# Fused block attention, MLP and mixture of experts: every maximum, exponential, copy and group of turns of the attention as a task of its own

## The chip, the cores and the metric

The kernel runs on one core of a Trainium2 chip. The metric is device time in microseconds, the median of several runs; lower is better. TensorE (PE), VectorE (DVE), ScalarE (ACT), GpSimd (POOL) and the DMA queue of SyncE (SP) run side by side, each through its own instructions in order, and wait for each other at semaphores. TensorE writes PSUM alone: eight banks of 128 x 512 f32 here.

## The reference, cut to what matters

```python
def _attn_ref(q, k, v):                   # 4 batches, 8 heads, 576 tokens, 64 features
    scores = np.matmul(q, k.transpose(0, 1, 3, 2)) / np.sqrt(D)
    scores = np.where(block_i >= block_j, scores, -1e9)     # blocks of 64 tokens
    attn = np.exp(scores - scores.max(-1))
    return np.matmul(attn / (attn.sum(-1) + 1e-09), v)
x = attention as (2304, 512)
x = leaky_relu(x @ w_in) @ w_out                            # 512 -> 2048 -> 512, weights are float64
P = 8 rounds of row and column normalisation of exp(x @ w_gate - max)
out = sum over 8 experts of P[:, e] * (relu(x @ w1[e]) @ w2[e])
```

## The kernel before, in words

Attention works on pairs of heads: 16 pairs p, two heads of 64 features side by side on the 128 partitions. Query blocks i = 0 to 8 of 64 tokens see keys 0 to 64(i + 1). For a pair, `scores(p, ...)` makes the products of some query blocks in banks of `ps_sc` (four banks; block 8 takes two, the others one), VectorE takes the negated row maxima into `nmax`, and ScalarE writes the exponentials to `ex` with their row sums to `ssum`. `turn_attn(p, g)` then transposes `ex` on TensorE in seven groups g, four 128x128 turns in a bank of `ps_tr` (two banks; group 6 is one turn, in `av`), and copies them to `at`: on VectorE for g = 1 and 5, on ScalarE for the others. `weigh(p, c, ...)` multiplies `at` by chunk c of the values into `av` (one buffer of two banks): `first_product` is chunk 0, `other_parts` are chunks 1 to 4. `split_x(p)` divides by the row totals (two VectorE products with `by_feature`) and splits the result in a high part (ScalarE cast) and a low part (GpSimd). The totals take a way through DRAM: `totals` (GpSimd, a VectorE reciprocal, two `row` DMAs) and `spread_totals` (four DMAs that read `row` back, spread over partitions, to `by_feature`).

`turn_q`, `turn_k` and `turn_tail` transpose the queries and keys of a later pair in banks of `ps_tr`; `spread` copies them to `qT` on ScalarE, `place_k` to `kT` on VectorE.

The loop over p is a software pipeline. In round p the list `turns` names the work in order: `prv` is pair p - 1, `cur` p, `nxt` p + 1 (scores) and `fol` p + 2 (turns of q and k). Attention stands in `manual_schedule` for TensorE, VectorE and ScalarE: these three run it in the program's order, and GpSimd and SP in an order that a planner sets. Each helper traces its products, maxima, exponentials and copies together, so the list's order is that of whole helpers.

Beside it, `steps` are the 72 steps that turn the first dense weights from float64 to two f32 parts: a load, six VectorE steps, one ScalarE step, two GpSimd instructions in one step, for each of eight units. One is taken behind each `scores`, five a round. After attention come the dense layers, which TensorE's queue may begin between the last rounds' instructions.

Of the kernel before, what the change touches and what calls it, by code (L numbers as in the profile page):

```python
# [8 lines left out]
F32 = mybir.dt.float32  # L9
F32R = mybir.dt.float32r  # L10
U32 = mybir.dt.uint32
AF = mybir.ActivationFunctionType
ALU = mybir.AluOpType
AX = mybir.AxisListType

P = 128
BLK = 64
# [19 lines left out]
def block_attention_mlp_moe(  # L37
# [15 lines left out]
    nc = tc.nc  # L53
    B, H, S, D = q.shape
# [3 lines left out]
    NQ = S // BLK  # L58
# [8 lines left out]
    TAIL = S - NFULL * P  # L67
# [147 lines left out]
    def attention(att, ps_sc, ps_tr, ps_av):  # L215
# [11 lines left out]
        off = [P * sum(nch[:i]) for i in range(NQ)]  # L227
        ew = P * sum(nch)
        ex = [att.tile([P, ew], F32, name=f"ex{i}") for i in range(2)]
        nmax = [att.tile([P, NQ + 1], F32, name=f"nmax{i}") for i in range(2)]  # L230
        ssum = [att.tile([P, NQ + 1], F32, name=f"ssum{i}") for i in range(2)]
        rsum = [att.tile([P, 2, (NQ + 1) // 2], F32, name=f"rsum{i}") for i in range(2)]
        NPAR = ((NQ + 1) // 2, NQ // 2)
        by_feature = [[att.tile([P, BLK * n], F32, name=f"by_feature{i}{n}") for n in NPAR] for i in range(2)]
        xs = att.tile([P, S], F32, name="xs")
# [38 lines left out]
        W = NFULL * P  # L274

        def spread(p, src, lo, n):
            scale = 1.0 / float(D) ** 0.5
            nc.scalar.activation(
                out=qT[p % 2][:, lo * BLK:(lo + n) * BLK], in_=src[:, 0:n * BLK], func=AF.Copy, scale=scale
            )  # L280

        def place_k(p, src, lo, hi):
            nc.vector.tensor_copy(out=kT[p % 2][:, lo:hi], in_=src)  # L283

        av = {}

        def av_tile(p):
            if p not in av:
                av[p] = ps_av.tile([P, 1024], F32, name="av", tag="av")
            return av[p]  # L290

        def turn_q(p):
            qm = ps_tr.tile([P, 512], F32, name="qm", tag="tr")
            for t in range(NFULL):
                nc.tensor.transpose(qm[:, t * P:(t + 1) * P], qraw[:, t, :], ident)
            spread(p, qm, 0, W // BLK)

        def turn_k(p):
            km = ps_tr.tile([P, 512], F32, name="km", tag="tr")
            for t in range(NFULL):  # L300
                nc.tensor.transpose(km[:, t * P:(t + 1) * P], kraw[:, t, :], ident)
            place_k(p, km[:, 0:W], 0, W)

        def turn_tail(p):
            tail = ps_tr.tile([P, 512], F32, name="qk_tail", tag="tr")
            nc.tensor.transpose(tail[:, 0:2 * TAIL], tails, ident)
            spread(p, tail, W // BLK, TAIL // BLK)
            place_k(p, tail[:, TAIL:2 * TAIL], W, S)

        latest = [None]
        crossed = range(1, NQ, 2)

        def scores(p, *members):
            nm, sm = nmax[p % 2], ssum[p % 2]
            work = []
            for i in members:
                n = BLK * (i + 1)
                cuts = [(0, n)] if n <= 512 else [(0, n // 2), (n // 2, n)]  # L320
                work.append((i, [
                    (lo, hi, ps_sc.tile([P, 512], F32, name="sc", tag="sc")[:, 0:hi - lo]) for lo, hi in cuts
                ]))
            for i, parts in work:
                for lo, hi, sc in parts:
                    for h in range(2):
                        r, o = slice(h * D, (h + 1) * D), (1 - h if i in crossed else h) * BLK
                        nc.tensor.matmul(  # L328
                            sc[o:o + BLK, :], qT[p % 2][r, i * BLK:(i + 1) * BLK], kT[p % 2][r, lo:hi],
                            start=True, stop=True,  # L330
                        )
            for i, parts in work:
                for s, (lo, hi, sc) in enumerate(parts):
                    latest[0] = nc.vector.tensor_reduce(  # L334
                        out=nm[:, i + s:i + s + 1], in_=sc, axis=AX.X, op=ALU.max, negate=True
                    )
                x = nm[:, i:i + 1]
                if len(parts) > 1:
                    nc.vector.tensor_tensor(out=x, in0=x, in1=nm[:, i + 1:i + 2], op=ALU.min)
                for s, (lo, hi, sc) in enumerate(parts):  # L340
                    nc.scalar.activation(  # L341
                        out=ex[p % 2][:, off[i] + lo:off[i] + hi], in_=sc, func=AF.Exp,
                        bias=x, scale=1.0, accum_out=sm[:, i + s:i + s + 1],
                    )
                if len(parts) > 1:
                    nc.gpsimd.tensor_tensor(
                        out=sm[:, i:i + 1], in0=sm[:, i:i + 1], in1=sm[:, i + 1:i + 2], op=ALU.add
                    )

        rows = {}  # L350

# [20 lines left out]
        def turn_attn(p, g):  # L372
            todo = order[4 * g:4 * g + 4]
            n = len(todo)
            if n == 1:
                tr = av_tile(p)[:, P:2 * P].rearrange("p (s h q) -> p s h q", s=1, h=2)
            else:
                tr = ps_tr.tile([P, 4, 2, BLK], F32, name="tr", tag="tr")
            for s, (i, c) in enumerate(todo):
                nc.tensor.transpose(  # L380
                    tr[:, s].rearrange("p h q -> p (h q)"),
                    ex[p % 2][:, off[i] + c * P:off[i] + (c + 1) * P],
                    swap if i in crossed else ident,
                )
            dst = at[:, 4 * g:4 * g + n]
            if g not in (1, 5):
                nc.scalar.copy(out=dst, in_=tr[:, 0:n])  # L387
            else:
                nc.vector.tensor_copy(out=dst, in_=tr[:, 0:n])

        o = 512 - P

        def weigh(p, c, h, part):
# [6 lines left out]
            else:  # L400
# [3 lines left out]
                    start=c == 0, stop=c == NKC - 1,  # L404
                )

        def split_x(p):
            b, hp = divmod(p, NPAIR)
            t = av.pop(p)
            for c, n in enumerate(NPAR):  # L410
                nc.vector.tensor_tensor(  # L411
                    out=xs.rearrange("p (i q) -> p i q", q=BLK)[:, c:NQ:2],
                    in0=t[:, o:o + S].rearrange("p (i q) -> p i q", q=BLK)[:, c:NQ:2],
                    in1=by_feature[p % 2][c].rearrange("p (q i) -> p i q", i=n), op=ALU.mult,
                )
            t0, t1 = b * S, (b + 1) * S
            cuts = [t0, XCUT, t1] if t0 < XCUT < t1 else [t0, t1]
            for u0, u1 in zip(cuts, cuts[1:]):
                hi, lo = x_parts(hp, u0, u1)
                y = xs[:, u0 - t0:u1 - t0]  # L420
                nc.scalar.copy(out=hi, in_=y)  # L421
                nc.gpsimd.tensor_tensor(out=lo, in0=y, in1=f32(hi), op=ALU.subtract)
# [7 lines left out]
        def first_product(p):  # L430
            for f, *a in first_part:
                f(p, *a)

        turns = [
            ("nxt", scores, 8), ("cur", turn_attn, 0), *other_parts[0:2],
            ("nxt", scores, 3, 2), *other_parts[2:], ("nxt", load_v), ("cur", turn_attn, 1), ("prv", split_x),
            ("nxt", scores, 5, 4), ("cur", totals), ("cur", turn_attn, 2), ("fol", turn_q),
            ("nxt", scores, 1, 0), ("fol", turn_tail), ("cur", first_product), ("cur", turn_attn, 3),
            ("nxt", scores, 7, 6), ("fol", turn_k), ("cur", turn_attn, 4), ("cur", turn_attn, 5),
            ("cur", turn_attn, 6), ("cur", spread_totals),  # L440
        ]
        opening = [
            ("nxt", scores, 1, 0), ("nxt", scores, 3, 2), ("nxt", scores, 5, 4), ("nxt", scores, 8),
            ("fol", turn_q), ("nxt", scores, 7, 6), ("nxt", load_v), ("fol", turn_k), ("fol", turn_tail),
        ]

        nc.gpsimd.memset(still, 0.0)
# [9 lines left out]
                nc.gpsimd.tensor_copy(out=t[:, off[i] + BLK * (i + 1):off[i] + P * nch[i]], in_=nought[:, 0:BLK])  # L457
        for t in vraw:
            nc.gpsimd.tensor_copy(out=t[TAIL:, NFULL, :], in_=nought[TAIL:, :])
        turn_q(0)  # L460
        turn_k(0)
        turn_tail(0)
        warm(ps_sc, "sc", 3)
        load_qk(1)
        steps = bits_list(
# [1 line left out]
        )  # L467
        for p in range(-1, NP + 1):
            who = {"prv": p - 1, "cur": p, "nxt": p + 1, "fol": p + 2}
            if p == NP:  # L470
                first_product(p - 1)
            for w, f, *a in (turns if p >= 0 else opening):
                if 0 <= who[w] < NP and (f is not first_product or p < NP - 1):
                    f(who[w], *a)
                if f is scores and p >= 0 and steps:
                    with ExitStack() as queued:
                        if p + 1 < NP:
                            queued.enter_context(tc.issue_after(getattr(latest[0], "ins", latest[0])))
                        steps.pop(0)()
            if p + 3 < NP:  # L480
                load_qk(p + 3)
        assert not steps
# [873 lines left out]
```

## Time and profile before

| | |
|---|---|
| median of 3 runs | 2120.01 us (2118.21 to 2121.92) |
| the profiled execution's own time | 2123.31 us |
| its span | 2121.5 us |
| TensorE busy, of the span | 2063.2 us (97%) |
| VectorE, ScalarE, GpSimd busy | 1551.9, 823.8, 655.1 us |
| chain that ended last | PE 90%, DVE 4%, ACT 2% |

The shares are means over stages: attention ends at about 257 us, the rest is dense layers and experts. What an edit of attention is worth is read from its rounds, not from these shares. A TensorE row's length is modelled and overlaps the next one; the distance between starts is the time that a step takes.

### The profile page before, as it was taken

The numbers are of one execution on the slowest core, as the hardware profiler recorded it, in microseconds if no ns is written. First come the engines' busy times: TensorE is split into PE (matmuls) and PEld (weight loads), VectorE is DVE, ScalarE is ACT, GpSimd is POOL, SyncE is SP. The second block draws the span as 40 slices with busy tenths as digits, with TensorE's granted clock in tenths as the row PEclk, the third lists the DMA queues.
The fourth block names the chain that finished last, engine by engine and source line by source line (L and its number), as shares of the span: only waits on it lengthen the run. The fifth ranks groups of instructions, "written<-read, shape, count | busy, mean of one in ns | idle before, by whom it ended". The sixth has DMA issues, their size and how long they took to land.

```text
span 2121.5 us, 32380 instructions
## 1 busy us (share of the span) xinstructions
PE 2063.2 (97%) x11498; PEld 1850.6 (87%) x11498; DVE 1551.9 (73%) x2671; ACT 823.8 (39%) x1811; POOL 655.1 (31%) x639
## 2 busy tenths in 40 slices
PE   8878899999999999999999999999999999999999
PEld 4444489898889889899989999999999999999998
DVE  5566465656555977887788688888888688888886
ACT  5555433222234544454445333323233423333322
POOL 2212222213102445544552223333232332333322
PEclk9999999999999999999999999999999999999999
DMA  5333211111004978888889777777777777777772
GB/s 125 83 94 88 65 46 40 41 40 50 30 23 177 334 271 309 307 295 302 322 303 350 268 256 253 273 255 266 258 252 272 261 258 253 253 273 256 270 252 110
DMA packets 240609, 436.92 MB, mean 206 GB/s; under 512 B 80680, under 2 KB 121640, under 8 KB 240192
## 3 DMA queue, kind: packets, MB, share of 16 engines
q1 hardware_dynamic: 239248, 434.56, 59.5%
q8 instruction: 91, 1.49, 0.3%
q14 instruction: 70, 0.57, 0.1%
q10 hardware_dynamic: 1200, 0.30, 0.1%
HBM read 308.82 MB, written 125.95 MB: 205 GB/s over the span
## 4 chain that ended last, share of the span: by engine, by line
PE 90%; DVE 4%; ACT 2%; issue 1%; DMA 1%; POOL 1%; SPq 0%; POOLq 0%; DVEq 0%; ACTq 0%
PE h_ps L851 28%; PE o L1019 20%; PE o L1075 12%; PE h_ps L508 9%; PE o L528 9%; PE o L851 3%; PE av L402 2%; PE sc L328 2%; PE tr L380 2%; DVE nmax L334 1%; ACT ex L341 1%; DVE xs L411 1%; DVE kT L283 0%; ACT at L387 0%; ACT xhfirst L421 0%
## 5 line engine op out<-in xcount | busy, mean ns | idle before, releaser
L948 DVE TENSOR_TENSOR xa<-o,xa 128x384 f32<-128x384 f32 x392 | 215.9, 552 | 110.9 <-PE o L1019 106.9
L851 PE MATMUL h_ps<-xhS,w1h 128*128 128x384 f32 x768 | 257.5, 335 | 0.0
L851 PE MATMUL h_ps<-xhS,w1l 128*128 128x384 f32 x768 | 256.6, 334 | 0.0
L851 PE MATMUL h_ps<-xlS,w1h 128*128 128x384 f32 x768 | 256.6, 334 | 0.0
L948 POOL TENSOR_TENSOR xa<-xa 128x384 f32<-128x384 f32 x92 | 106.0, 1153 | 407.8 <-DVE xa L948 370.5
L948 ACT COPY places<-h_ps 128x384 f32<-128x384 f32 x192 | 92.3, 481 | 286.9 <-PE h_ps L851 219.4
L948 ACT CAST xllate<-xa 128x384 fp32r<-128x384 f32 x120 | 61.6, 513 | 279.6 <-POOL xa L948 279.6
L851 PE MATMUL h_ps<-xhA,w1h 128*128 128x384 f32 x448 | 150.7, 336 | 1.7 <-DVE c L868 1.7
L851 PE MATMUL h_ps<-xhA,w1l 128*128 128x384 f32 x448 | 149.9, 335 | 0.0
L851 PE MATMUL h_ps<-xlA,w1h 128*128 128x384 f32 x448 | 149.9, 335 | 0.0
L851 PEld LDWEIGHTS h_ps<-xhS,w1h 128*128 128x128 f32 x768 | 144.2, 188 | 0.7 <-issue 0.6
L851 PEld LDWEIGHTS h_ps<-xlS,w1h 128*128 128x128 f32 x768 | 144.2, 188 | 0.0
L851 PEld LDWEIGHTS h_ps<-xhS,w1l 128*128 128x128 f32 x768 | 144.1, 188 | 0.0
L1075 PE MATMUL o<-w2h,xhlate 128*128 128x512 f32 x408 | 143.8, 391 | 0.0
L948 POOL TENSOR_TENSOR places<-places 128x384 f32<-128x384 f32 x60 | 61.0, 1017 | 251.2 <-DVE wa L948 234.2
L1075 PE MATMUL o<-w2h,xllate 128*128 128x512 f32 x384 | 133.9, 389 | 0.0
L1019 PE MATMUL o<-xllate,w2h 128*128 128x384 f32 x480 | 122.6, 336 | 0.0
L1019 PE MATMUL o<-xhlate,w2h 128*128 128x384 f32 x480 | 121.8, 334 | 0.0
L765 POOL TENSOR_TENSOR wa<-wraw 128x256 f32<-128x256 f32 x32 | 29.0, 907 | 299.7 <-DVE w1l L783 262.9
L516 DVE TENSOR_TENSOR g<-h_ps,g 128x512 f32<-128x512 f32 (+1 forms) x80 | 50.8, 635 | 91.6 <-ACT g L515 91.3
L528 PE MATMUL o<-hh,w2h 128*128 128x512 f32 (+1 forms) x320 | 117.8, 369 | 0.0
L528 PE MATMUL o<-hh,w2l 128*128 128x512 f32 (+1 forms) x320 | 117.7, 368 | 0.0
(257 smaller groups left out, 5719.7 us busy)
## 6 DMA issues: line engine op xcount, KB each, us to landing
wraw<-in_moe_w_dram SPq DMA_DIRECT2D x64, 512.0 KB, 4.5
w1h<-k_1h SPq DMA_DIRECT2D x64, 512.0 KB, 5.1
w1l<-k_1l SPq DMA_DIRECT2D x64, 512.0 KB, 6.3
w2h<-k_1h SPq DMA_DIRECT2D x60, 512.0 KB, 6.1
w2l<-k_1l SPq DMA_DIRECT2D x60, 512.0 KB, 6.9
w1h<-k_0h SPq DMA_DIRECT2D x64, 384.0 KB, 4.1
w1l<-k_0l SPq DMA_DIRECT2D x64, 384.0 KB, 4.7
w2h<-k_0h SPq DMA_DIRECT2D x60, 384.0 KB, 3.9
```

The lines of the kernel that those rows point to most:

```text
L328: nc.tensor.matmul(sc[o:o + BLK, :], qT[p % 2][r, i * BLK:(i + 1) * BLK], kT[p % 2][r, lo:hi], start=True, stop=True,)
L334: latest[0] = nc.vector.tensor_reduce(out=nm[:, i + s:i + s + 1], in_=sc, axis=AX.X, op=ALU.max, negate=True)
L380: nc.tensor.transpose(tr[:, s].rearrange("p h q -> p (h q)"), ex[p % 2][:, off[i] + c * P:off[i] + (c + 1) * P], swap if i in crossed else ...
L402: nc.tensor.matmul(av[p][r, 512 + P * max(c - 1, 0):512 + S - P], lhsT, a[:, q0:, :], start=c == 0, stop=c == NKC - 1,)
L508: nc.tensor.matmul(ps[:, 0:n], w[:, c, cols], x, start=c == 0 and s == 0, stop=c == KC - 1 and s == 2,)
L516: nc.vector.tensor_tensor(out=g[:, 0:n], in0=ps[:, 0:n], in1=g[:, 0:n], op=ALU.max)
L528: nc.tensor.matmul(ps[:, 0:n], w[:, cut], h[:, 0:n], start=start and m == 0, stop=stop and m == 2)
L765: nc.gpsimd.tensor_tensor(out=one[:, 0], in0=a21, in1=a22, op=ALU.add)
L851: mm = nc.tensor.matmul(ps, w[:, c], x[:, c], start=first and c == 0 and s == 0, stop=c == 1 and s == 2, skip_group_check=True,)
L948: ins = f(*a, **k)
L1019: mm = nc.tensor.matmul(o, a, b, start=i == 0, stop=i == 5)
L1075: mm = nc.tensor.matmul(o, h, w, start=m == 0, stop=m == 11)
```

## The change

Helpers are cut in two: one that fills a bank and one that takes it (`turn_q` and `take_q`, `turn_attn` and `take_attn`, `score_products` and `peak`, `peak_whole`, `weights`; `split_x` gives its two products to `scale_x`). The list `turns` names each by itself, in a new order; `turn_k` stands right behind `turn_q`, ahead of `first_product`. Group 0 is turned after group 1, group 5 before group 4. `convert` stands at five places of its own. The last pair's `first_product` stands in its own round like the others. The opening keeps its order through `block` and `take_turns`.

```diff
+        held = {}
         def turn_q(p):
-            qm = ps_tr.tile([P, 512], F32, name="qm", tag="tr")
+            qm = held["q"] = ps_tr.tile([P, 512], F32, name="qm", tag="tr")
             ...
-            spread(p, qm, 0, W // BLK)
+        def take_q(p):
+            spread(p, held.pop("q"), 0, W // BLK)
...
+        def take_k(p):
+            place_k(p, held.pop("k")[:, 0:W], 0, W)
...
+        def take_q_tail(p):
+            spread(p, held["tail"], W // BLK, TAIL // BLK)
+        def take_k_tail(p):
+            place_k(p, held.pop("tail")[:, TAIL:2 * TAIL], W, S)
...
+        def peak(p, i, s=0):
+            latest[0] = nc.vector.tensor_reduce(
+                out=nmax[p % 2][:, i + s:i + s + 1], in_=score[i][s][2], axis=AX.X, op=ALU.max, negate=True
+            )
+        def peak_whole(p, i):
+            x = nmax[p % 2][:, i:i + 2]
+            nc.vector.tensor_tensor(out=x[:, 0:1], in0=x[:, 0:1], in1=x[:, 1:2], op=ALU.min)
+        def weights(p, i, s=0):
+            lo, hi, sc = score[i][s]
+            sm = ssum[p % 2]
+            nc.scalar.activation(
+                out=ex[p % 2][:, off[i] + lo:off[i] + hi], in_=sc, func=AF.Exp,
+                bias=nmax[p % 2][:, i:i + 1], scale=1.0, accum_out=sm[:, i + s:i + s + 1],
+            )
+            if s:
+                nc.gpsimd.tensor_tensor(out=sm[:, i:i + 1], in0=sm[:, i:i + 1], in1=sm[:, i + 1:i + 2], op=ALU.add)
...
+        def take_attn(p, g):
+            tr = held.pop(("tr", g))
+            dst = at[:, 4 * g:4 * g + tr.shape[1]]
             if g not in (1, 5):
-                nc.scalar.copy(out=dst, in_=tr[:, 0:n])
+                nc.scalar.copy(out=dst, in_=tr)
             else:
-                nc.vector.tensor_copy(out=dst, in_=tr[:, 0:n])
+                nc.vector.tensor_copy(out=dst, in_=tr)
...
+        def convert(p):
+            if steps:
+                with tc.issue_after(getattr(latest[0], "ins", latest[0])):
+                    steps.pop(0)()
         turns = [
-            ("nxt", scores, 8), ("cur", turn_attn, 0), *other_parts[0:2],
-            ("nxt", scores, 3, 2), *other_parts[2:], ("nxt", load_v), ("cur", turn_attn, 1), ("prv", split_x),
-            ("nxt", scores, 5, 4), ("cur", totals), ("cur", turn_attn, 2), ("fol", turn_q),
-            ("nxt", scores, 1, 0), ("fol", turn_tail), ("cur", first_product), ("cur", turn_attn, 3),
-            ("nxt", scores, 7, 6), ("fol", turn_k), ("cur", turn_attn, 4), ("cur", turn_attn, 5),
-            ("cur", turn_attn, 6), ("cur", spread_totals),
+            ("nxt", score_products, 8), *other_parts[0:2], ("nxt", peak, 8, 1), ("nxt", peak, 8, 0),
+            ("cur", convert), ("nxt", score_products, 3, 2), ("nxt", peak_whole, 8), ("nxt", peak, 2),
+            ("cur", turn_attn, 1), ("nxt", weights, 8, 0), ("nxt", weights, 8, 1), ("nxt", weights, 2),
+            ("cur", totals), ("cur", take_attn, 1), *other_parts[2:], ("nxt", load_v), ("cur", turn_attn, 0),
+            ("cur", turn_attn, 2), ("cur", take_attn, 0), ("nxt", score_products, 5, 4), ("cur", convert),
+            ("prv", scale_x, 0), ("nxt", peak, 3), ("fol", turn_q), ("cur", take_attn, 2), ("prv", scale_x, 1),
+            ("nxt", peak, 4), ("nxt", weights, 3), ("fol", take_q), ("fol", turn_k), ("nxt", peak, 5),
+            ("fol", take_k), ("nxt", weights, 4), ("cur", convert), ("cur", first_product),
+            ("nxt", score_products, 1, 0), ("nxt", weights, 5), ("fol", turn_tail), ("nxt", peak, 0),
+            ("cur", turn_attn, 3), ("nxt", peak, 1), ("cur", convert), ("fol", take_q_tail),
+            ("nxt", score_products, 7, 6), ("nxt", weights, 0), ("fol", take_k_tail), ("cur", turn_attn, 5),
+            ("cur", take_attn, 3), ("nxt", weights, 1), ("prv", split_x), ("cur", convert),
+            ("cur", turn_attn, 4), ("nxt", peak, 6), ("nxt", peak, 7), ("nxt", weights, 6),
+            ("cur", take_attn, 5), ("nxt", weights, 7), ("cur", take_attn, 4), ("cur", turn_attn, 6),
+            ("cur", take_attn, 6),
+            ("cur", spread_totals),
         ]
```

## Rows read from the trace of the kernel before

**Rows 1.** The page, its first line.
```profile
span 2121.5 us, 32380 instructions
```

**Rows 2.** Stretches: length, busy PE, PEld, DVE, ACT, POOL, PEclk, DMA share, GB/s.
```profile
14.34:26.42 12.08, 10.02 (x83) 5.54 (x83) 7.12 (x20) 7.76 (x26) 0.74 (x3) 1.00 0.54 127
26.42:241.64 215.22, 172.16 (x1275) 87.95 (x1274) 126.30 (x279) 117.01 (x375) 45.59 (x57) 0.91 0.37 88
241.64:256.58 14.94, 12.44 (x90) 5.73 (x90) 7.13 (x17) 7.51 (x25) 4.17 (x4) 0.89 0.27 70
256.58:300.00 43.42, 43.42 (x221) 34.32 (x222) 21.30 (x39) 16.24 (x30) 9.02 (x9) 1.00 0.10 27
```

**Rows 3.** TensorE's waits, 26.42 to 241.64 us: total, times, longest.
```profile
PE qk_tail L306 <- ACT at L387: 27.8, 13, 2.6
PE tr L380 <- DVE kT L283: 15.3, 13, 1.5
```

**Rows 4.** Busy time in two rounds, columns as in rows 2.
```profile
167.89:184.50 16.61, 13.47 (x98) 6.93 (x98) 10.25 (x23) 8.82 (x30) 2.22 (x4) 0.90 0.29 69
184.50:199.44 14.94, 11.92 (x98) 6.33 (x99) 9.26 (x23) 9.34 (x31) 4.92 (x7) 1.00 0.49 119
```

**Rows 5.** Timeline of ScalarE: start us, us, instruction, idle before.
```profile
182.13 0.51 ACT L421 CAST xhfirst<-xs 128x384 fp32r<-128x384 f32 x1 [2.16 <-DVE xs L411]
...
183.87 0.58 ACT L387 COPY at<-tr 128x512 f32<-128x512 f32 x1
```

**Rows 6.** Timeline of VectorE: the maxima of blocks 7 and 6.
```profile
187.59 1.22 DVE L334 TENSOR_REDUCE nmax<-sc 128x1 f32<-128x512 f32 x2 [1.11 <-PE sc L328]
```

**Rows 7.** Timeline of TensorE in the round at clock 1.00.
```profile
184.50 0.33 PE L306 MATMUL qk_tail<-ident,tails 128*128 128x128 f32 x1 [2.12 <-ACT at L387]
184.76 0.44 PE L399 MATMUL av<-at,vraw 128*64 128x128 f32 x4
...
185.88 0.33 PE L380 MATMUL tr<-swap,ex 128*128 128x128 f32 x1
...
186.47 1.08 PE L328 MATMUL sc<-kT,qT 64*64 64x512 f32 x8
...
190.16 1.19 PE L328 MATMUL sc<-kT,qT 64*64 64x288 f32 x8
191.28 0.33 PE L380 MATMUL tr<-ident,ex 128*128 128x128 f32 x1
...
191.87 0.97 PE L402 MATMUL av<-at,vraw 128*64 128x448 f32 x4
192.77 0.65 PE L328 MATMUL sc<-kT,qT 64*64 64x256 f32 x8
193.35 1.20 PE L402 MATMUL av<-at,vraw 128*64 128x320 f32 x12
194.48 0.33 PE L380 MATMUL tr<-ident,ex 128*128 128x128 f32 x1
...
195.07 0.86 PE L328 MATMUL sc<-kT,qT 64*64 64x384 f32 x8
195.86 0.44 PE L380 MATMUL tr<-ident,ex 128*128 128x128 f32 x2
...
196.35 0.60 PE L295 MATMUL qm<-ident,qraw 128*128 128x128 f32 x4
196.88 0.44 PE L328 MATMUL sc<-kT,qT 64*64 64x128 f32 x8
```

**Rows 8.** ScalarE's exponentials, 26.42 to 241.64 us: busy, mean ns, idle before.
```profile
L341 ACT ACTIVATE ex<-sc,nmax 128x288 f32<-128x288 f32 (+8 forms) x130 | 64.1, 501 | 43.5 <-DVE nmax L334 21.7 <-DVE nmax L339 19.9 <-DVE wb L176 1.9
```

**Rows 9.** Timelines of GpSimd and VectorE, where they meet.
```profile
160.10 1.29 POOL L202 TENSOR_TENSOR w2l<-wa,wraw 128x512 fp32r<-128x512 f32 x1
...
160.34 1.06 DVE L339 TENSOR_TENSOR nmax<-nmax 128x1 f32<-128x1 f32 x1
```

**Rows 10.** DMA issues, 26.42 to 241.64 us: count, size, median us to landing.
```profile
by_feature<-row SPq DMA_DIRECT2D x26, 80.0 KB, 2.8
```

More of the change, by code (lines that the diff above doesn't have):

```diff
@@ L290, in av_tile, with score_products @@
             return av[p]
+        held = {}
         def turn_q(p):
-            qm = ps_tr.tile([P, 512], F32, name="qm", tag="tr")
+            qm = held["q"] = ps_tr.tile([P, 512], F32, name="qm", tag="tr")
             for t in range(NFULL):
                 nc.tensor.transpose(qm[:, t * P:(t + 1) * P], qraw[:, t, :], ident)
-            spread(p, qm, 0, W // BLK)
+        def take_q(p):
+            spread(p, held.pop("q"), 0, W // BLK)
         def turn_k(p):
-            km = ps_tr.tile([P, 512], F32, name="km", tag="tr")
+            km = held["k"] = ps_tr.tile([P, 512], F32, name="km", tag="tr")
             for t in range(NFULL):
                 nc.tensor.transpose(km[:, t * P:(t + 1) * P], kraw[:, t, :], ident)
-            place_k(p, km[:, 0:W], 0, W)
+        def take_k(p):
+            place_k(p, held.pop("k")[:, 0:W], 0, W)
         def turn_tail(p):
-            tail = ps_tr.tile([P, 512], F32, name="qk_tail", tag="tr")
+            tail = held["tail"] = ps_tr.tile([P, 512], F32, name="qk_tail", tag="tr")
             nc.tensor.transpose(tail[:, 0:2 * TAIL], tails, ident)
-            spread(p, tail, W // BLK, TAIL // BLK)
-            place_k(p, tail[:, TAIL:2 * TAIL], W, S)
+        def take_q_tail(p):
+            spread(p, held["tail"], W // BLK, TAIL // BLK)
+        def take_k_tail(p):
+            place_k(p, held.pop("tail")[:, TAIL:2 * TAIL], W, S)
         latest = [None]
         crossed = range(1, NQ, 2)
-        def scores(p, *members):
-            nm, sm = nmax[p % 2], ssum[p % 2]
-            work = []
+        score = {}
+        def score_products(p, *members):
             for i in members:
@@ L320, in scores @@
                 cuts = [(0, n)] if n <= 512 else [(0, n // 2), (n // 2, n)]
[L321 to L325, printed above, removed]
+                score[i] = [(lo, hi, ps_sc.tile([P, 512], F32, name="sc", tag="sc")[:, 0:hi - lo]) for lo, hi in cuts]
+            for i in members:
+                for lo, hi, sc in score[i]:
                     for h in range(2):
@@ L331, in scores @@
                         )
[L332 to L348, printed above, removed]
+        def peak(p, i, s=0):
[14 more added lines that the diff above has]
+                nc.gpsimd.tensor_tensor(out=sm[:, i:i + 1], in0=sm[:, i:i + 1], in1=sm[:, i + 1:i + 2], op=ALU.add)
         rows = {}
@@ L384, in turn_attn @@
                 )
-            dst = at[:, 4 * g:4 * g + n]
+            held["tr", g] = tr[:, 0:n]
+        def take_attn(p, g):
+            tr = held.pop(("tr", g))
+            dst = at[:, 4 * g:4 * g + tr.shape[1]]
             if g not in (1, 5):
-                nc.scalar.copy(out=dst, in_=tr[:, 0:n])
+                nc.scalar.copy(out=dst, in_=tr)
             else:
-                nc.vector.tensor_copy(out=dst, in_=tr[:, 0:n])
+                nc.vector.tensor_copy(out=dst, in_=tr)
         o = 512 - P
@@ L405, in weigh, with scale_x @@
                 )
+        def scale_x(p, c):
+            n = NPAR[c]
+            nc.vector.tensor_tensor(
+                out=xs.rearrange("p (i q) -> p i q", q=BLK)[:, c:NQ:2],
+                in0=av[p][:, o:o + S].rearrange("p (i q) -> p i q", q=BLK)[:, c:NQ:2],
+                in1=by_feature[p % 2][c].rearrange("p (q i) -> p i q", i=n), op=ALU.mult,
+            )
+            if c:
+                del av[p]
         def split_x(p):
             b, hp = divmod(p, NPAIR)
[L409 to L415, printed above, removed]
             t0, t1 = b * S, (b + 1) * S
@@ new lines, in attention, with block @@
+            ("cur", spread_totals),
+        ]
+        def block(*members):
+            takes = [("nxt", score_products, *members)]
+            for i in members:
+                takes.append(("nxt", peak, i))
+                if i == NQ - 1:
+                    takes += [("nxt", peak, i, 1), ("nxt", peak_whole, i)]
+                takes.append(("nxt", weights, i))
+                if i == NQ - 1:
+                    takes.append(("nxt", weights, i, 1))
+            return takes
+        take_turns = [("fol", turn_q), ("fol", take_q)], [
+            ("fol", turn_k), ("fol", take_k), ("fol", turn_tail), ("fol", take_q_tail), ("fol", take_k_tail)
@@ L441, in attention @@
         ]
         opening = [
-            ("nxt", scores, 1, 0), ("nxt", scores, 3, 2), ("nxt", scores, 5, 4), ("nxt", scores, 8),
-            ("fol", turn_q), ("nxt", scores, 7, 6), ("nxt", load_v), ("fol", turn_k), ("fol", turn_tail),
+            *block(1, 0), *block(3, 2), *block(5, 4), *block(8), *take_turns[0], *block(7, 6), ("nxt", load_v),
+            *take_turns[1],
         ]
@@ L459, in attention @@
             nc.gpsimd.tensor_copy(out=t[TAIL:, NFULL, :], in_=nought[TAIL:, :])
-        turn_q(0)
-        turn_k(0)
-        turn_tail(0)
+        for f in (turn_q, take_q, turn_k, take_k, turn_tail, take_q_tail, take_k_tail):
+            f(0)
         warm(ps_sc, "sc", 3)
@@ L469, in attention @@
             who = {"prv": p - 1, "cur": p, "nxt": p + 1, "fol": p + 2}
-            if p == NP:
-                first_product(p - 1)
             for w, f, *a in (turns if p >= 0 else opening):
-                if 0 <= who[w] < NP and (f is not first_product or p < NP - 1):
+                if 0 <= who[w] < NP:
                     f(who[w], *a)
[L475 to L479, printed above, removed]
             if p + 3 < NP:
```

## The prediction

> **What bounds the kernel now.** I first read the page's first line, then the busy times of stretches, to find what the edited stage is worth. The profiled execution took 2123.31 us by its own time, 1.8 us more than its span [rows 1], and stands 3.30 us above the median of the runs, 2120.01. The edit touches attention alone. From 256.58 us on TensorE has no idle time (43.42 us busy of 43.42 [rows 2]), and it does the dense layers in its order until the end. So a microsecond taken out ahead of 256.58 us should come off the end, and one taken off another engine is worth nothing by itself.
>
> In attention the steady stretch is 26.42 to 241.64 us: thirteen rounds of the pair loop (p = 1 to 13), 215.22 / 13 = 16.56 us each. TensorE is busy for 13.24 us of a round, VectorE for 9.72, ScalarE for 9.00, GpSimd for 3.51, and TensorE's granted clock averages 0.91 [rows 2]. No engine is full, so something waits. The list of TensorE's waits has only two entries, each once in every round [rows 3]: `qk_tail` for a ScalarE copy, 27.8 us in all (2.14 a round), and a transpose for VectorE's copy of `kT`, 15.3 us in all (1.18). Together 3.32 us a round.
>
> The third loss is the clock. Set two rounds side by side, each from one `qk_tail` to the next [rows 4]: at mean clock 0.90 a round took 16.61 us, at 1.00 it took 14.94 with the same instructions, so a fall to the lower level (1.2 GHz) costs 1.67 us. The falls come after the wait for `qk_tail`. In the round at 1.00 TensorE was busy for 11.92 us: that is the work of a round at 2.4 GHz. The three parts add up: 11.92 + 3.32 + about 1.3 (1.67 in most rounds, none in some) = 16.5.
>
> Why the two waits? `qk_tail` needs a bank of `ps_tr` that `turn_attn(2)` filled. Its copy on ScalarE stands in line behind `split_x`'s casts, which sat idle for 2.16 us until VectorE had made `xs`, and behind two exponentials: the cast starts at 182.13 us, the copy only at 183.87 [rows 5], while TensorE had ended `scores(1, 0)` at about 182.4. The other is alike: `turn_attn(5)` wants the bank of `turn_k`, and the copy to `kT` stands behind the two maxima of blocks 7 and 6 (1.22 us [rows 6]), placed one line above it. Neither engine is short of time; its order is wrong.
>
> **The change part by part.** Nothing is added to or taken from the arithmetic: the same products, turns, maxima, exponentials, copies, five conversion steps a round, and the same DMAs. So instruction costs sum to zero, and what matters is whether the new order leaves a bank free when TensorE comes back to it. TensorE's own steps, from start to next start at full clock [rows 7]: score 8 takes 1.12 us, a group of four turns 0.59 (0.49 behind other turns), `weigh` of chunk 1 0.90, score 3 and 2 0.58, `weigh` of the other chunks 1.13, score 5 and 4 0.79, `turn_q` 0.53 (`turn_k` the same), `first_product` 1.12, score 1 and 0 0.44, the tail 0.26, score 7 and 6 about 1.08. From these comes, for each bank, how long TensorE is elsewhere between filling it and wanting it again.
>
> *Banks of `ps_tr`* (two, nine uses a round). The shortest returns are `turn_attn(0)` to `turn_q`, with `turn_attn(2)` and score 5 and 4 between: 0.49 + 0.79 = 1.28 us; `turn_attn(2)` to `turn_k`: 0.79 + 0.53 = 1.32; `turn_attn(3)` to `turn_attn(4)`: 1.08 + 0.49 = 1.57; the tail to `turn_attn(5)`: 0.59 + 1.08 = 1.67; `turn_attn(1)` to `turn_attn(2)`: 1.13 + 0.59 = 1.72. Against them stands one copy, 0.58 us [rows 5], and two hand-overs. I put a hand-over at 0.1 us (an estimate: rows 6 has a maximum start at 187.59, the products before it starting at 186.47 and taking 1.08). So a copy that starts on time leaves 0.5 us to spare at the tightest place. What stood ahead of the copies is gone: `split_x`'s casts come after `take_attn(3)`, and `take_k` comes ahead of all of that round's later maxima. One thing may stand there, a ScalarE conversion of about one copy's length in one step of nine, and it about eats the 0.5. Both waits go: -3.32 us a round.
>
> *Banks of `ps_sc`* (four). Score 5 and 4 take the banks of 8: TensorE is away for 0.90 + 0.58 + 0.59 + 1.13 + 0.59 + 0.49 = 4.28 us, against two maxima and a minimum, a conversion and two exponentials at 0.50 [rows 8] or, with maxima as in rows 6 and a conversion as long as one, at most 1.2 + 0.6 + 0.2 + 1.0 + hand-overs = 3.3. Score 3 and 2 take the banks of 7 and 6: 0.49 + 0.49 + 0.2 + 1.12 + 0.90 = 3.2 us against two maxima (1.22) and two exponentials (about 1.2, half hidden by the second maximum) = 2.2. Score 7 and 6 take those of 5 and 4 after 0.53 + 0.53 + 1.12 + 0.44 + 0.26 + 0.59 = 3.47. All have 0.9 us or more to spare.
>
> *`av`* (one buffer). `first_product` of a pair now follows `scale_x` of the pair before it by position. On VectorE, from the end of `weigh` (4.3 us after the round's start) come `scale_x(0)`, a maximum, `scale_x(1)`: about 1.8 us, done at 6.1; TensorE wants the bank at 7.3. Free.
>
> *Moved on POOL and SP.* `totals` moves ahead of `take_attn(1)`, so VectorE's reciprocal now waits for GpSimd early in the round; GpSimd has 3.51 us of work in 12 and its sums of the last round are due 2 us earlier. `load_v`, `spread_totals` and the `load_qk` DMAs keep their number; SP's own order isn't written by hand. Cost taken 0, bound under the rivals.
>
> *`peak_whole`* is a 128x1 minimum on VectorE that gates both exponentials of block 8. It was 0.16 us unhindered and 1.06 in the row at 160.34, with GpSimd inside a 1.29 us instruction that began at 160.10 [rows 9]. Where they meet again the exponentials come 0.9 us late, and the 1.0 us spare (4.28 - 3.3) hides it: 0. The Trainium skill (SBUF — State Buffer, Who interferes with whom) says that a VectorE instruction with two SBUF inputs is blocked, not slowed, while GpSimd reads SBUF. The trace agrees as far as one instruction goes; if both of GpSimd's conversion instructions were sat out (about 2.6 us), some 1.5 us would be lost in seven of the rounds, an estimate of 10 us, and the sum would be 2067 instead of 2057.
>
> **Sum.** A round's floor is 11.92 us; the ceiling is 16.56 (waits come back elsewhere). With every return covered I take 12.1: the floor and 0.2 for the rounds in which a conversion sits in the way. At no more than 0.5 us of wait at a time the clock should stay at 1.0, as it does through the rest of rows 7 and in rows 2 after 256.58.
> - Thirteen rounds: 13 x (16.56 - 12.1) = 58.0 us (bounds 0 and 60.3).
> - Round 0 (14.34 to 26.42): 12.08 us with 10.02 busy at full clock [rows 2]. The opening's order on each engine is unchanged, and its exponentials arrive late, so I take 10.8: 1.3 us (0 to 2.06).
> - Round 14 (241.64 to 256.58): 14.94 us at clock 0.89 [rows 2]; it has no `turn_q`, `turn_k`, tail: 11.92 - 1.32 = 10.6 of work. I take 11.4: 3.5 us (0 to 4.3).
>
> In all 62.8 us: 2123.31 - 62.8 = 2060.5, and for the median of runs 2057. At the floors 66.7 us: 2053.
>
> **The rivals.**
> *VectorE sets the pace.* For it: 9.72 us of work in one fixed order with some dozen waits on TensorE, and it sat idle for (215.22 - 126.30) / 13 = 6.84 us of a round. If 3.3 of that stays, a round is 13.0 us: 13 x 3.56 + 3 = 49 us, 2071. Against it: the conversions now stand where it has nothing else to do.
>
> *The clock keeps falling.* A copy misses the 0.5 us, a wait of half a microsecond stays, and the round drops to the lower level as before: 12.0 + 0.5 + 1.67 = 14.2 us, 13 x 2.4 + 3 = 34 us, 2086. The Trainium skill (TensorE: Matmul & The Clock Gate, A second HAM failure mode: psum-queue depth-cycling) tells of a kernel whose short idle times between groups kept the clock going up and down. Against it here: in the round at 1.00 the wait of about 1 us for `kT` did no harm to the clock [rows 4].
>
> *Given back in the dense layers.* The first products there might want weights or tokens that aren't ready when TensorE comes 63 us earlier. The 72 conversion steps still end in round 14 at five a round. If the last weight unit were still owed, its nine steps are 1.8 rounds of 12.1 us, 22 us: 2079.
>
> *Slower: the spread of the totals comes late.* `scale_x` now stands ahead of eight other VectorE tasks and of `first_product`. It needs `by_feature`: after the reciprocal (about 3.2 us into a round) the `row` DMAs, then, behind `load_v` on SP, four issues that land 2.8 us later [rows 10]. By order of issue I put that at 10 us in all, an estimate; the rows are wanted 13 us after the reciprocal. Every microsecond of delay past those 3, and past the 1.2 that `av` has to spare, adds one to each round; past 8.7 (3 + 1.2 + 4.46) the kernel is slower. At 10 us late: 13 x 1.3 = 17 us more, 2137. Against it: SP stands still for part of every round now, and in no row did VectorE wait for these rows.
>
> **How the numbers follow.** Chances: forecast 0.66, VectorE 0.14, clock 0.11, given back 0.04, late totals 0.05 (of which 0.03 is slower and 0.01 no change). The forecast's own range is 2051 (floors, less the spread of 2 us that the runs show) to 2065 (a round of 12.7). With the VectorE case and its neighbours the range is 2051 to 2079, which leaves out the clock case, most of the late totals and some of the given back: 0.2. Faster by over 0.2% (about 4 us, what a measurement of this kernel can tell from no change) 0.95, within 0.2% 0.02, slower 0.03.
>
> **What would show it.** Right: waits of `qk_tail` and of the turn after `turn_k` gone from TensorE's list, starts of `qk_tail` 12.1 us apart, granted clock 1.00 between 26 us and the first dense product, which comes near 194 us. Wrong in order: a new entry in that list over 0.3 us a round, on `qm`, `km` or `sc`; VectorE without idle time; VectorE idle on `by_feature`; idle TensorE after the first dense product.

## The result, and the profile after

The changed kernel takes 2061.28 us (median of 4 runs, 2059.65 to 2063.41) against 2120.64 us for the kernel before: ratio 0.9722, 95% interval [0.9705, 0.9739]. The forecast was 2057, range 2051 to 2079. Profiled execution against profiled execution it is 2060.68 against 2123.31, 62.6 us less; the sum had 62.8. By medians it is 59.4 us: the profiled execution before was slower than its median (2123.31 against 2120.64), so the match to 0.2 us is in part luck.

The stretches that answer to [rows 2], columns as there, from one round's first score product to the next and then to the end:

```profile
14.65:25.42 10.77, 9.45 (x83) 5.46 (x83) 6.65 (x19) 6.29 (x22) 0.49 (x2) 1.00 0.48 114
25.42:183.45 158.03, 150.21 (x1276) 82.06 (x1275) 120.62 (x280) 118.17 (x376) 41.14 (x57) 1.00 0.50 121
183.45:194.99 11.54, 10.55 (x90) 5.37 (x89) 7.42 (x18) 9.14 (x30) 4.74 (x6) 1.00 0.22 58
194.99:2058.90 1863.91, 1857.91 (x9975) 1743.00 (x9975) 1405.41 (x2331) 683.52 (x1360) 602.61 (x555) 1.00 0.63 222
```

Thirteen rounds take 158.03 us, 12.16 each, where they took 16.56. The granted clock is 1.00 throughout. From the first dense product to the end it is 1863.91 us; in the kernel before, that stretch (256.58 to 2121.5) is 1864.92 long. So what attention gained comes off the end whole.

TensorE's waits in those thirteen rounds, the list that answers to [rows 3]:

```profile
PE av L414 <- ACT at L399: 7.8, 13, 0.9
```

Both old entries are gone. One new one stands there, not in the prediction: 0.6 us a round at `weigh` of chunk 1, for a ScalarE copy to `at`. The end of a round on TensorE (start us, length, instruction, idle before) and on ScalarE:

```profile
85.97 0.27 PE L388 MATMUL av<-ident,ex 128*128 128x128 f32 x1
86.18 1.19 PE L334 MATMUL sc<-kT,qT 64*64 64x288 f32 x8
87.95 0.97 PE L414 MATMUL av<-at,vraw 128*64 128x448 f32 x4 [0.58 <-ACT at L399]
```
```profile
85.86 0.64 ACT L351 ACTIVATE ex<-sc,nmax 128x448 f32<-128x448 f32 x1
...
86.48 0.68 ACT L351 ACTIVATE ex<-sc,nmax 128x512 f32<-128x512 f32 x1
...
87.14 0.58 ACT L399 COPY at<-tr 128x512 f32<-128x512 f32 x1
87.61 0.28 ACT L399 COPY at<-av 128x128 f32<-128x128 f32 x1
```

The group-6 turn was made at 85.97 us, early, but its copy is the last of ScalarE's round, behind two exponentials and the copy of group 4. It ends at 87.89, and `weigh` begins at 87.95.

### The profile page after: what moved, and what is told of

Its sections match the earlier page's. It is cut to its first block, busy times and chain, and to the rows that moved or that the text cites. A ratio compares the mean times of both kernels' runs of the same rounds, so it can differ in the third digit from the quotient of the medians.

```text
span 2058.9 us, 32391 instructions
## 1 busy us (share of the span) xinstructions
PE 2039.9 (99%) x11498; PEld 1844.3 (90%) x11498; DVE 1547.8 (75%) x2671; ACT 825.3 (40%) x1811; POOL 652.6 (32%) x639
## 4 chain that ended last, share of the span: by engine, by line
PE 94%; DVE 3%; ACT 2%; DMA 1%; issue 1%; SPq 0%; POOL 0%; DVEq 0%; ACTq 0%; POOLq 0%
PE h_ps L888 30%; PE o L1056 21%; PE o L1112 13%; PE h_ps L545 10%; PE o L565 10%; PE o L888 3%; PE av L414 2%; PE sc L334 2%; PE tr L388 2%; ACT ex L351 1%; ACT at L399 0%; DVE xa L985 0%; DVE nmax L340 0%; PE qm L297 0%; DVE w1l L820 0%
```

## The experiments

Ratios are to the kernel before, run on the same chip beside it. Where two kernels that did not run beside each other are compared, it is by their ratios; 0.001 of the time is 2.1 us. The first five kernels are the changed kernel with edits, the last four the kernel before with edits.

**The new wait: whose end does `weigh` want?** `group6_first` swaps two copies:

```diff
-            ... ("nxt", weights, 7), ("cur", take_attn, 4), ("cur", turn_attn, 6),
-            ("cur", take_attn, 6),
+            ... ("nxt", weights, 7), ("cur", turn_attn, 6), ("cur", take_attn, 6),
+            ("cur", take_attn, 4),
```

> The changed kernel with one swap in ScalarE's order: the copy of group 6 (the one that reads av) ahead of the copy of group 4. The changed kernel's TensorE waits 0.58 us once a round, at weigh of chunk 1, until ScalarE's last copy. Theory A (that product writes the av tile, so it waits for the copy that reads group 6's turn out of the same tile): the copy ends one copy earlier, about 0.48 us, the wait falls to about 0.1, the round from 12.16 to about 11.7, 14 x 0.48 = 7 us: 2054. Theory B (it waits until every copy to at is done, group 4's among them): the wait stays at 0.58 and the time at 2061.

Measured: 2054.86 us, 0.9680 [0.9666, 0.9693]. The wait is gone from the list in all rounds but one (0.4 us). These rows settle who was waited for, TensorE's and ScalarE's:

```profile
83.25 1.19 PE L334 MATMUL sc<-kT,qT 64*64 64x288 f32 x8
84.53 0.97 PE L414 MATMUL av<-at,vraw 128*64 128x448 f32 x4
```
```profile
84.22 0.26 ACT L399 COPY at<-av 128x128 f32<-128x128 f32 x1
84.36 0.60 ACT L399 COPY at<-tr 128x512 f32<-128x512 f32 x1
```

The product starts at 84.53, just after the copy out of `av` (84.48) and well before the copy of group 4 ends (84.96). It starts 1.28 us after score 8; in `exp7_last` below, where the copy out of `av` ends earlier in the round, it starts 1.11 us after (105.59 and 106.70), so some 0.16 us of wait is left here, up to the end of that copy. Theory A holds, B falls: the product writes the `av` tile and waits for the reader of that tile, though by the code the two use different columns (512 to 959 and 128 to 255).

`exp7_last` takes the copies out from behind the last exponential too:

```diff
-            ("cur", take_attn, 5), ("nxt", weights, 7), ("cur", take_attn, 4), ("cur", turn_attn, 6),
-            ("cur", take_attn, 6),
+            ("cur", take_attn, 5), ("cur", take_attn, 4), ("cur", turn_attn, 6), ("cur", take_attn, 6),
+            ("nxt", weights, 7),
```

> The changed kernel with both copies, group 4's and then group 6's, ahead of the exponential of block 7, which becomes ScalarE's last task of a round. Theory A and B alike: the copies end 0.66 us earlier, the wait at weigh of chunk 1 goes, a round takes 11.6 us, 14 x 0.55 = 8 us: 2053. Rival: the exponential of block 7, now 0.75 us later, holds the bank that score 3 wants, and a wait of 0.2 to 0.5 us comes up there instead: 2056 to 2061.

Measured: 2053.96 us, 0.9676 [0.9663, 0.9689]; the interval lies wholly below the changed kernel's, so this version beats that one too; it can't be told apart from `group6_first`. No wait for block 7's exponential came up in the rounds. From 25 to 180 us TensorE is busy for all but 0.2 us:

```profile
105.59 1.19 PE L334 MATMUL sc<-kT,qT 64*64 64x288 f32 x8
106.70 0.97 PE L414 MATMUL av<-at,vraw 128*64 128x448 f32 x4
```
```profile
25.00:180.00 155.00, 154.81 (x1320) 85.02 (x1318) 124.51 (x289) 121.50 (x389) 45.74 (x61) 1.00 0.53 125
```

**One bank missed, and the clock.** `casts_back` puts the casts back ahead of a copy:

```diff
-            ("prv", scale_x, 0), ("nxt", peak, 3), ("fol", turn_q), ("cur", take_attn, 2), ("prv", scale_x, 1),
+            ("prv", scale_x, 0), ("nxt", peak, 3), ("fol", turn_q), ("prv", scale_x, 1), ("prv", split_x), ("cur", take_attn, 2),
...
-            ("cur", take_attn, 3), ("nxt", weights, 1), ("prv", split_x), ("cur", convert),
+            ("cur", take_attn, 3), ("nxt", weights, 1), ("cur", convert),
```

> The changed kernel with split_x's casts put back ahead of the copy of group 2, right behind scale_x. Theory (a copy that stands behind a cast that waits for VectorE misses its bank): scale_x ends about 4.9 us after the round's first score product, cast 0.6, copy 0.58, and turn_k wants the bank about 0.8 us before that: a wait of 0.8 us on turn_k a round, clock still 1.00, 14 x 0.8 = 11 us: 2072. Rival 1 (the lower clock comes with any wait): 0.8 + 1.67 a round, 2096. Rival 2 (the round is paced by the chain that ends in the wait at weigh of chunk 1, and swallows it): 2061 to 2064.

Measured: 2071.91 us, 0.9762 [0.9749, 0.9775], which is 0.0040 or 8.5 us more than the changed kernel. Its waits and clock (first two rows: total, times, longest; 25 to 240 us):

```profile
PE av L414 <- ACT at L399: 8.8, 15, 0.7
PE km L305 <- ACT at L399: 7.9, 13, 0.7
```
```profile
25.00:180.00 155.00, 140.76 (x1176) 75.49 (x1176) 110.10 (x256) 108.81 (x347) 40.48 (x54) 1.00 0.49 114
```

The wait is where it was expected, on `km`, 0.61 us a round for the 0.8 that was expected. In the round of this row of ScalarE, the cast and its wait for `xs` put the copy behind it off by about 1.1 us:

```profile
108.34 0.67 ACT L436 CAST xhfirst<-xs 128x576 fp32r<-128x576 f32 x1 [0.51 <-DVE xs L421]
```

Two waits of some 0.6 us a round leave the granted clock at 1.00: rival 1 falls, and rival 2 too, since the other wait didn't shrink.

**`turn_k` in the middle of the pair.** `k_late` puts it back:

```diff
-            ... ("fol", take_q), ("fol", turn_k), ("nxt", peak, 5),
-            ("fol", take_k), ("nxt", weights, 4), ...
+            ... ("fol", take_q), ("nxt", peak, 5),
+            ("nxt", weights, 4), ...
-            ("nxt", score_products, 7, 6), ("nxt", weights, 0), ("fol", take_k_tail), ("cur", turn_attn, 5),
+            ("nxt", score_products, 7, 6), ("nxt", weights, 0), ("fol", take_k_tail), ("fol", turn_k), ("fol", take_k), ("cur", turn_attn, 5),
```

> The changed kernel with turn_k and its copy at their old place behind score 7 and 6, the copy still ahead of the maxima of 6 and 7. Theory (its place is not what counts, the copy's place in VectorE's line is): a wait of 0.3 to 0.4 us comes up at group 4's turns, whose bank is turn_k's, and the end of the round shifts as TensorE has 0.5 us more to do after score 7 and 6 but VectorE 0.6 more ahead of the maxima: 0.1 to 0.6 us a round, 2062 to 2069. Rival (k's turn in the middle of the pair is what removed the old wait): the old 1.18 us a round comes back, 2077 or more.

Measured: 2083.86 us, 0.9817 [0.9804, 0.9830]: 0.0095 or 20 us of the gain lost, more than the theory gave, in the rival's size but not at its place:

```profile
PE av L414 <- ACT at L399: 20.5, 14, 2.1
PE tr L388 <- DVE kT L283: 4.5, 13, 0.3
```

The wait for `kT` is the 0.35 a round that was worked out. The larger part is the wait for `av`, grown from 0.6 to 1.5 us a round, 12 us in all; the clock fell a little too (0.99 from 25 to 180 us). VectorE shows why the wait grew:

```profile
90.52 0.69 DVE L283 COPY kT<-km 128x512 f32<-128x512 f32 x1 [1.55 <-PE km L305]
91.13 1.12 DVE L154 TENSOR_SCALAR wa<-wraw 128x512 uint32<-128x512 uint32 x1
92.18 1.21 DVE L340 TENSOR_REDUCE nmax<-sc 128x1 f32<-128x448 f32 x2
```

The products of 7 and 6 began at 88.82 us; their maxima begin at 92.18, behind the copy and a conversion. Exponentials, copies and `weigh` follow in a chain. If that is the cause, freeing the copies from the exponentials should give most of it back. `k_late_copies_first` is `k_late` with

```diff
+            ("cur", take_attn, 5), ("cur", take_attn, 4), ("cur", turn_attn, 6), ("cur", take_attn, 6),
+            ("nxt", weights, 6), ("nxt", weights, 7),
```

as the round's end in place of exponentials first.

> The run k_late (turn_k and its copy back behind score 7 and 6) with ScalarE's copies of groups 4 and 6 ahead of the exponentials of 6 and 7. Theory (k's late place costs 22 us mainly because take_k and a conversion stand ahead of the maxima of 6 and 7, whose exponentials stand ahead of the copy that frees av for weigh of chunk 1): with the copies no longer behind those exponentials the wait of 1.5 us at weigh goes, 0.35 us for kT's copy stays, a round is 11.55 + 0.35 = 11.9, and the time about 2058. Rival (k's late place costs by itself): the exponentials of 6 and 7 come so late that score 3 or group 1's turns wait for them, and it stays above 2070.

Measured: 2060.70 us, 0.9715 [0.9701, 0.9729]. The `kT` wait stays, the `av` wait is gone from all rounds but one:

```profile
PE tr L388 <- DVE kT L283: 4.5, 13, 0.3
PE av L414 <- ACT at L399: 0.8, 1, 0.8
```

Putting the copies first gives 0.0102 or 22 us with `turn_k` late. But it gives 0.0046 or 10 us with `turn_k` early too (the changed kernel to `exp7_last`). So of the 20 us that `turn_k`'s late place costs, 0.0056 or 12 us went with the chain ahead of the copies, which is what the `av` wait had grown by. The other 0.0039 or 8 us stay against `exp7_last`; 4.5 of them are the wait for `kT`, the rest was not traced.

**How much of the gain is three moves?** In the kernel before, `before_casts_late` moves only the casts:

```diff
+        def cast_x(p):                       # the second half of split_x
...
-            ("nxt", scores, 1, 0), ("fol", turn_tail), ("cur", first_product), ("cur", turn_attn, 3),
+            ("nxt", scores, 1, 0), ("fol", turn_tail), ("cur", first_product), ("cur", turn_attn, 3),
+            ("prv", cast_x),
```

> The kernel before with one edit: split_x's two ScalarE casts stand behind the copy of group 3, its VectorE products stay. Theory P (the prediction's words: the copy of group 2 is late because the casts stand ahead of it): most of the wait of qk_tail goes, 2.1 us, and with it the lower clock, 1.3 us, 14 rounds: about 2073. Theory Q (the copy stands behind the exponentials of 5 and 4, these wait for maxima, and the maxima stand behind scale_x on VectorE): the exponentials start only 0.15 to 0.3 us earlier, qk_tail's wait falls from 2.14 to about 1.8: 2112 to 2118.

Measured: 2121.33 us, 0.9992 [0.9982, 1.0002]: no change. Theory P, the prediction's own words, falls. ScalarE after the edit:

```profile
183.01 0.58 ACT L341 ACTIVATE ex<-sc,nmax 128x384 f32<-128x384 f32 x1 [2.65 <-DVE nmax L334]
...
184.09 0.58 ACT L387 COPY at<-tr 128x512 f32<-128x512 f32 x1
```

It sits idle for 2.65 us until VectorE has the maxima, and only then come the exponentials and the copy. On VectorE the maxima stand behind `split_x`'s two products (`scale_x` in the changed kernel):

```profile
181.26 1.25 DVE L411 TENSOR_TENSOR xs<-av,by_feature 128x320 f32<-128x320 f32 x2
182.43 0.95 DVE L334 TENSOR_REDUCE nmax<-sc 128x1 f32<-128x384 f32 x2
```

`qk_tail`'s wait is 26.1 us in thirteen rounds, against 27.8, and that for `kT` grew from 15.3 to 17.4. Theory Q named the mechanism; it gave 2 to 8 us for the small shift, and what was measured (0.8 us by medians) is not clear of the noise.

`before_copy2_first` also puts the copy ahead of those exponentials; `before_k_first` puts `place_k` ahead of the maxima of 7 and 6; `before_both` does all three. TensorE's order is that of the kernel before in each:

```diff
-        def scores(p, *members):
+        def scores(p, *members, between=None):     # called between the products and the maxima
+            if between:
+                between()
...
+        def scores_turn(p, *members):              # before_copy2_first
+            scores(p, *members, between=lambda: turn_attn(p - 1, 2))
+        def scores_k(p, *members):                 # before_k_first
+            scores(p, *members, between=(lambda: turn_k(p + 1)) if p + 1 < NP else None)
```

> The kernel before with two edits: the casts late as in the run beside it, and group 2's turns and their copy traced between the products of score 5 and 4 and their maxima and exponentials, so that the copy stands ahead of those two exponentials; TensorE's order is unchanged. Theory Q: the copy starts when the turns end, qk_tail's wait goes, the next wait is group 3's turns for turn_q's copy, about 0.7 us, the clock stays at 1.00: 16.56 - 2.14 - 1.3 + 0.7 = 13.8 a round, 38 us: about 2082. Rival: without the split of all helpers another wait as long takes its place: above 2105.

Measured: 2089.53 us, 0.9849 [0.9835, 0.9864]. The wait of `qk_tail` is gone; group 3's turns wait for `turn_q`'s copy as worked out (0.64 us a round). The wait for `kT` grew from 1.18 to 1.47 us, and the clock fell in a few rounds (0.98 from 25 to 180 us), which theory Q had not foreseen: it gave some 8 us more gain than there was.

```profile
PE tr L385 <- DVE kT L283: 20.6, 14, 1.9
PE tr L385 <- ACT qT L278: 8.3, 13, 1.1
```

> The kernel before with one edit: turn_k and its copy traced between the products of score 7 and 6 and their maxima, so VectorE copies kT ahead of those maxima; TensorE's order is unchanged. Theory: the wait of 1.18 us for kT falls to about 0.3, 14 x 0.9 = 12 us, the wait of qk_tail and the clock stay as they are: 2108. Rival: the maxima and exponentials of 7 and 6 come 0.6 us later and hold score 3's banks, so that half or more is given back: 2114 to 2121.

Measured: 2111.74 us, 0.9954 [0.9939, 0.9969]. The wait for `kT` falls to 0.35 us a round; that of `qk_tail` is unchanged at 27.8 us. Two small ones come up (3.0 and 1.5 us in all). The theory's 12 us is 10.

```profile
PE qk_tail L306 <- ACT at L392: 27.8, 13, 2.6
PE tr L385 <- DVE kT L283: 4.5, 13, 0.3
```

> The kernel before with the three edits of the other runs together (casts late, copy of group 2 ahead of the exponentials of 5 and 4, copy of kT ahead of the maxima of 7 and 6). Theory (two late copies and the clock that falls with them are nearly the whole loss): both waits gone but for 0.3 and 0.7 us, clock 1.00, a round of 11.92 + 1.0 = 12.9: 13 x 3.6 + 2 = 49 us, 2071. Rival (only tasks of their own for all maxima, exponentials and copies do it): above 2090.

Measured: 2075.59 us, 0.9787 [0.9772, 0.9802]. With these waits left the clock stays at 1.00:

```profile
PE tr L388 <- ACT qT L278: 8.3, 13, 1.1
PE tr L388 <- DVE kT L283: 4.9, 14, 0.3
PE tr L388 <- DVE at L397: 3.0, 10, 0.4
PE av L410 <- ACT at L395: 1.5, 4, 0.8
```

So three moved tasks give 0.0213 of the change's 0.0278, some three quarters. Apart they give 0.0151 and 0.0046; the 0.0016 that is lacking to the whole is not clear of the noise. The last quarter, 0.0065 or 14 us, is for the larger part waits: those listed above are 17.7 us, and the changed kernel has 8.4 in the same stretch (25 to 240 us). The rest is in part TensorE's new order, some 0.2 us a round (below). Which of the other moves takes it out was not tried one by one.

## Why the prediction was right, point by point

*What bounds the kernel.* Right: the two waits and the clock. The dense stretch kept its length to 1.0 us, so the rival "given back" falls.

*A round of 12.1 us.* It is 12.16, by errors that nearly cancel, which is luck. The floor was put at 11.92 us of TensorE work, and it is 150.21 / 13 = 11.55. Groups of turns now stand side by side, and a group behind other turns takes 0.49 us, not 0.59, as [rows 7] had shown: that is about 0.2 of the 0.37 (an estimate). The rest is how busy time is counted: the last row before a wait counts up to its modelled end, which elsewhere lies under the next row, and the kernel before had two such rows in a round, the changed one has one. The 0.2 for conversions in the way was too much: two rounds of the thirteen are longer than the others, by 0.13 and 0.27 us. And 0.58 us of waiting in every round was not foreseen.

*The step that failed* is the one on `av` ("Free"). It looked at `first_product` and `scale_x` alone. `av` has another use in a round, group 6's turn, and so another return: from that turn to `weigh` of chunk 1 TensorE has only score 8, 1.12 us, while ScalarE has two exponentials and a copy ahead of the copy that frees it. The prediction listed the returns of every bank of `ps_tr` and `ps_sc` and left out this one, the shortest. Put at nothing, it cost 7.8 us of waiting in the thirteen rounds; `group6_first`, with hardly any of it, is 0.0042 or 9 us faster.

*Why the old waits stood there.* Half wrong. The copy of group 2 was late, as said, but not by the casts: moving them alone changed nothing. The two exponentials ahead of it, which the prediction names beside the casts, waited for maxima behind `split_x`'s products. The forecast came out since the change moves the copy ahead of the exponentials too, which gives most of the gain in `before_copy2_first`. For `kT` the reason given holds (`before_k_first`).

*Banks of `ps_tr` and `ps_sc`.* Right: no wait on `qm`, `km`, `tr` or `sc` in the thirteen rounds. The margin of about half a microsecond is real: in `casts_back` a copy put off by about 1.1 us leaves 0.6 us of wait.

*The clock.* Right, and the clock case falls: neither one wait of 0.58 us nor two of about 0.6 brought the lower level. The Trainium skill (TensorE: Matmul & The Clock Gate, A second HAM failure mode: psum-queue depth-cycling) has short idle times between groups taking the clock down. Idle times of this size did not do so here.

*`peak_whole` beside GpSimd.* It cost nothing, but not for the reason given: its sixteen executions took 153 to 161 ns, so none was held up and there was nothing for the 1.0 us to hide. The two hardly met. Once, VectorE's instruction began within the last 0.14 us of a GpSimd instruction's row, whose end is rough:

```profile
123.53 1.26 POOL L201 TENSOR_TENSOR wa<-wa,w2h 128x512 f32<-128x512 f32 x1
```
```profile
124.65 0.16 DVE L346 TENSOR_TENSOR nmax<-nmax 128x1 f32<-128x1 f32 x1
```

So the rule of the Trainium skill (SBUF — State Buffer, Who interferes with whom) had no clear occasion in them, and the 10 us worked out from it didn't come.

*Rounds 0 and 14.* 10.77 us for 10.8; 11.54 for 11.4.

*Late totals, VectorE.* VectorE waited about 0.2 us a round at `scale_x`, 2.9 us in all, of which 1.1 is put down to a DMA: no landing came late enough to matter. It was busy for 120.62 of 158.03 us, and with `exp7_last` TensorE is full: VectorE doesn't set the pace.

## What to carry to other kernels

Where engines run a fixed order, list for every buffer the time that the filling engine is elsewhere between filling it and wanting it again, and set it against all that stands ahead of the copy that frees it; a tile that has two uses in a round has two such returns, and the one left out is the one that costs. Trace the chain ahead of a late copy to its first link before moving something: the task next to it on its engine may itself be waiting, and moving it gives nothing. A task put ahead of a chain that has nothing to spare delays the whole chain, and can cost more than its own length: the late place of `turn_k` cost some 1.5 us a round, for a copy of 0.69 us.

## What the runs showed of the hardware that was not expected

A product waits for a copy that reads other columns of the PSUM tile it writes. In `group6_first` the same product does not wait for a copy that writes other columns of the SBUF tile `at` that it reads: it starts at 84.53 us, and the copy of group 4 ends at 84.96. The runs show when the product starts, not why the wait is set so; whether the two could overlap was not tried.

At waits of about 0.6 us, even two in a round of some 13 us, the granted clock stayed at 1.00. In `k_late`, with 1.5 us a round on average at one place, it averaged 0.99 from 25 to 180 us, and before, with 2.1 us, 0.91. In `k_late` it fell in two rounds, behind waits of 2.08 and 1.83 us; the first:

```profile
109.16 0.97 PE L414 MATMUL av<-at,vraw 128*64 128x448 f32 x4 [2.08 <-ACT at L399]
```

From 111 to 114 us the granted clock is 0.50, the lower level. A wait of that length did not always bring it: before, the round at 184.50 [rows 7] follows one of 2.12 us and stays at 1.00.
